# Sparse attention and FFN on one core: in units 14 to 23 the transfer engine turns the probabilities of all four head pairs

## The chip, the cores and the metric

One core of a Trainium2 chip. The metric is device time in microseconds, the median of three runs. The engines are TensorE (PE), VectorE (DVE), ScalarE (ACT), GpSimd (POOL) and SyncE (SP), which here only issues transfers; 16 DMA engines carry them.

## What is computed

```python
B, H, S, D = q.shape                  # 4, 8, 768, 64
scores = scale * np.matmul(q, k.transpose(0, 1, 3, 2))
mask = np.abs(blk_i - blk_j) <= window            # blocks of 32, window 1
mask = mask | (blk_i == 0) | (blk_j == 0) | (blk_i == n_blocks - 1) | (blk_j == n_blocks - 1)
...                                               # and 3 sampled blocks per block of queries
scores = np.where(mask, scores, -1000000000.0)
attn = softmax(scores)
x = (attn @ v) as [3072, 512]
h = x @ w_in                                      # 512 x 2048
g = np.where(h > 0.0, h, np.exp(np.minimum(h, 0.0)) - 1.0)
out = g @ w_out                                   # 2048 x 512
```

## The kernel before

The 3072 tokens are 24 **units** of 128 (`u` = 0 to 23), four blocks of 32 queries each. Units 8 and 20 hold the first and last blocks of a pair of batches, which attend to all keys; a head pair there has three tiles of keys, elsewhere one. Two units together make the tokens of one round of the FFN, **U** = 0 to 11 (U = 10 has units 20 and 21). Numbers are kept as two fp16 parts, a high and a low one.

`attention(u, t, via)` does this for a unit: Q is loaded and turned (qT, and qS with halves swapped), keys are gathered (kG, on POOL) and rows of V (VT, loads on SP and an indirect one on POOL). Then, for each of the four head pairs `hp` and each of its tiles: the scores on PE (line 788, into s), the row maximum on DVE (799), the exponential on ACT (817, into e), the cast to fp16 (p, high part), the subtraction that gives the low part (822, the second half of p), the **turn** of p into pT, and the product with V on PE (837, into w or av), 32 matmuls for a tile. Sums of those go to x; after the last pair the unit is normed, cast and subtracted (xn) and turned into xT, on which the FFN works. There are two e tiles, two p tiles and four pT tiles.

`turn16` makes a turn in one of two ways. By "PE" it is eight 128x128 transposes on TensorE (line 385) into a PSUM tile (the tag av, or s in units 8 and 20), which ACT or DVE then copies to pT (lines 297 and 299). By "DMA" it is one transpose by the transfer engine that SP issues (line 377), from p in SBUF to pT in SBUF. Which way a pair goes is the middle entry of `via`: pairs with `hp < via[1]` go by PE. Before, that is 4 for units 0 to 3 and `PP` = 2 for all others; their Q and xn go by DMA.

`ffn(U, t)` has eight steps `f2`: two groups of 12 matmuls for h (line 885, 256 columns each), three operations for the activation on ACT and DVE (895, 897, 893), cast and subtraction to g, and two groups of 6 matmuls into o (line 908, 512 columns). At the end of a U two tiles ro leave PSUM, and SP stores them (642); a U has two such stores, and there is one ro tile.

No engine chooses its work at run time. `Plan.add` notes every operation with the engines it may run on and a due time; `Plan.order` lets a model of the chip run, starts on each engine the earliest due operation that is ready in the model, with assumed durations, and writes the instructions in that order. Attention of a U has due times 130 (`LEAD`) ahead of its FFN, so the operations of later units lie between the FFN's matmuls of earlier tokens. On the chip each engine, and SP, then works strictly in the written order and waits where something is not there yet. A turn by DMA stands in the model as 1.3 on SP, 2.4 of transfer and 2.5 until it has landed:

```python
        if via == "DMA":
            plan.add({"SP": 1.3}, t, lambda e: nc.sync.dma_start_transpose(dst(), flat(src.ap)),
                     r=[src], new=new, w=w, dma=2.4, name=name)
            return
...
                turn16(t + PITCH * hp + TURN, p, lambda pT=pT: pT.ap, "PE" if hp < via[1] else "DMA", new=[pT], name=f"pt{u}.{hp}", bank=bank)
```

Of the kernel before, what the change touches and what calls it, by code (L numbers as in the profile page):

```python
# [225 lines left out]
def kernel(  # L226
# [44 lines left out]
    def buf(tag, shape, dtype, pool=None):  # L271
        def make():
            made[0] += 1
            return (pool or sb).tile(
                shape, dtype, tag=tag, bufs=rooms[tag], name=f"{tag}{made[0]}")
        return Buf(tag, make)
# [203 lines left out]
    def zero_rows(prio):  # L480
        z = buf("st4", [P, 2 * RW], F16)
        plan.add({"POOL": 0.6}, prio, lambda e: nc.gpsimd.memset(z.ap[0:BLK, :], 0.0), new=[z], name="zero")
        for g in range(NPAIR):
            for n in (0, NB - 1):
                for d, xs in vd[g]:
                    def put(e, d=d, xs=xs, n=n):
                        nc.sync.dma_start(d.ap[n * BLK : (n + 1) * BLK, :], z.ap[0:BLK, 0 : RW * len(xs)])
                    plan.add({"SP": 0.45}, prio, put, r=[z], new=[d] if n == 0 else [],
                             w=[d] if n else [], dma=0.3, name=f"z{g}")
# [26 lines left out]
    def spare(prio, n):  # L516

        got = []
        for _ in range((n + 1) // 2):
            vt = Buf("VT", lambda: None)  # L520

            def take(e, vt=vt):
                vt.slot = next_slot()
                in_room["v", vt.slot] = None
            plan.add({"SP": 0.01}, prio, take, new=[vt], name="spare")
            for half in range(2):
                got.append((Buf(None, lambda vt=vt, half=half: VT[
                    :, 2 * vt.slot + half].rearrange("p b (h x) -> p b h x", x=VW)), [vt]))
        return got
# [46 lines left out]
    def keys(g, x, c, prio, via="DMA"):  # L576
        s, n = buf("st2", [P, H, D], F32), buf("n2", [P, H, 2, D], F16)
        plan.add({"SP": 0.45}, prio, lambda e: nc.sync.dma_start(
            s.ap, k[2 * g + x][:, c * P : (c + 1) * P, :].rearrange("h p d -> p h d")),
            new=[s], dma=1.35, name=f"k{g}.{c}")  # L580
        split(prio, s, n, lambda: n.ap[:, :, 0, :], lambda: n.ap[:, :, 1, :], KS, True, f"k{g}.{c}")
        turn16(prio, n, lambda: kT[x][:, :, c * P : (c + 1) * P], via, w=[kT_buf[x][c]],
               name=f"kt{g}.{c}")

    def values(g, c, prio):
        n = buf("st4", [P, 2, H, VW], F16)
        ends(n, prio, f"v1{g}.{c}")
        for x in range(2):
            s = buf("st2", [P, H, D], F32)
            plan.add({"SP": 0.45}, prio, lambda e, s=s, x=x: nc.sync.dma_start(  # L590
                s.ap, v[2 * g + x][:, c * P : (c + 1) * P, :].rearrange("h p d -> p h d")),
                new=[s], dma=1.4, name=f"v{g}.{c}")
            split(prio, s, n, lambda x=x: n.ap[:, x, :, D + 1 : VW - 1], lambda x=x: n.ap[:, x, :, 0:D],
                  VS, False, f"v{g}.{c}")
        pieces = {0: [(0, BLK, NB * BLK), (BLK, P, BLK)],
                  NKC - 1: [(0, P - BLK, c * P), (P - BLK, P, (NB + 1) * BLK)]}.get(c, [(0, P, c * P)])
        for p0, p1, row in pieces:
            def put(e, p0=p0, p1=p1, row=row):
                nc.sync.dma_start(
                    vd[g][0][0].ap[row : row + p1 - p0, :], n.ap[p0:p1].rearrange("p b h x -> p (b h x)"))  # L600
            plan.add({"SP": 0.45}, prio, put, r=[n], w=[vd[g][0][0]], dma=1.55 * (p1 - p0) / P, name=f"vs{g}.{c}")
# [324 lines left out]
    TWO, AHEAD, T, F0, LEAD, NPE = 6, 16.0, 58.0, 60.0, 130.0, 4  # L926
    WI, WID, F2, LAG = -100.0, 3.0, 4.5, 14.0
    V1, K1 = 70.0, 16.0
    QP, PP, XP = 0, 2, 0
    zero_rows(-480)  # L930
    room = [None, None, *spare(-490, 4)]
    for x in range(2):
# [8 lines left out]
    for U in range(NU // 2):  # L941
        t = F0 + T * U
        for u in (2 * U, 2 * U + 1):
            at = t - LEAD + (T / 2 if U else NEXT) * (u % 2)
            if u == NUP:
                for c in range(NKC):
                    for x in range(2):
                        keys(1, x, c, at - K1 + c, "PE")
                for c in range(NKC):
                    values(1, c, at - V1 + 5 * c)  # L950
            attention(u, at, ("PE", 4, "PE") if u < NPE else (("DMA", "PE")[QP], PP, ("DMA", "PE")[XP]))
        ffn(U, t)
    warm_up()
    tables()
# [30 lines left out]
```

## Time and profile before

| | us |
|---|---|
| median of three runs | 823.76 |
| the runs | 824.18, 820.37, 823.76 |
| span of the profiled execution | 807.9 |
| median less span | 15.9 |
| PE busy in the span | 711.3 |
| DVE, ACT, POOL busy | 506.4, 428.9, 392.7 |

The profile is one execution, and its span is counted from the first to the last instruction; the profiled execution's own whole time is not given apart from the runs, so the median stands for it. Busy times of PE are unions of matmuls that overlap in the array. A wait is put down to what ended it. SP and the DMA engines have no busy share of their own in the head of the page; what they do is read from the issues and from who waits for them.

### The profile page before, as it was taken

Reading aid. Unit: us, or ns where it says so; the run is one execution under the profiler, and the core shown is the slowest. Engines: PE = TensorE matmul, PEld = TensorE weight load, DVE = VectorE, ACT = ScalarE, POOL = GpSimd, SP = SyncE. Lnnn points to the kernel's source line nnn. Section 1 sums busy time; section 2 is a strip of 40 time slices with the busy share of each in tenths; the row PEclk is TensorE's granted clock in tenths of the full one; section 3 lists DMA queues with packets and bytes.
Section 4 is the critical chain, followed back from the end, with each engine's and each line's share of the span. In section 5 each row is a group of like instructions: output and inputs, shape, how many; then the busy total and the mean of one; then the engine's idle time right before and its main releaser. Section 6 shows DMA issues by size and latency. Waiting matters only on the chain.

```text
span 807.9 us, 26664 instructions
## 1 busy us (share of the span) xinstructions
PE 711.3 (88%) x11256; PEld 488.3 (60%) x11256; DVE 506.4 (63%) x854; ACT 428.9 (53%) x747; POOL 392.7 (49%) x600
## 2 busy tenths in 40 slices
PE   6445665999998999899899998999999999999993
PEld 3333553767657657567567656656667576566761
DVE  7689788998876747666478766647555566522210
ACT  4598777888545636355466525445345346322220
POOL 2587657687534347543565535445324464422120
PEclk8555578999999999999999999999999999999997
DMA  8898999988787789999459987464761698210000
GB/s 231 248 281 277 264 263 212 217 204 163 134 179 223 169 148 209 172 170 200 94 106 182 162 176 93 110 131 42 172 114 15 94 208 146 41 40 1 28 1 26
DMA packets 191064, 120.07 MB, mean 149 GB/s; under 512 B 148000, under 2 KB 168608, under 8 KB 190944
## 3 DMA queue, kind: packets, MB, share of 16 engines
q1 hardware_dynamic: 185664, 100.79, 61.0%
q0 software_dynamic: 5280, 17.58, 8.5%
q8 instruction: 88, 1.44, 0.8%
q14 instruction: 32, 0.26, 0.1%
HBM read 82.05 MB, written 13.21 MB: 118 GB/s over the span
## 4 chain that ended last, share of the span: by engine, by line
PE 66%; DMA 14%; DVE 6%; issue 4%; ACT 3%; POOL 2%; SPq 2%; POOLq 1%; DVEq 0%; ACTq 0%
PE o L908 27%; PE h L885 25%; PE s L788 5%; DMA out_dram<-ro 5%; PE w L837 3%; DMA pT<-p 2%; PE av L837 2%; DMA wo<-in_moe_w_out_dram 2%; DMA st<-in_k_dram 2%; PE av L385 2%; DMA VT<-vd 1%; PE s L385 1%; DMA st<-in_v_dram 1%; ACT e L817 1%; DVE w L451 1%
## 5 line engine op out<-in xcount | busy, mean ns | idle before, releaser
L885 PE MATMUL h<-xT,wi 128*128 128x256 f16 x2304 | 280.4, 275 | 7.8 <-DVE fe L893 4.7
L908 PE MATMUL o<-wo,g 128*128 128x512 f16 x1152 | 274.6, 381 | 0.0
L885 PEld LDWEIGHTS <-wi 128*128 128x128 f16 x2304 | 220.2, 98 | 53.9 <-issue 9.0
L902 POOL TENSOR_TENSOR g<-fe,g 128x512 f16<-128x512 f32 x79 | 96.0, 1215 | 188.8 <-DVE g L299 167.8
L908 PEld LDWEIGHTS <-g 128*128 128x128 f16 x1152 | 107.5, 98 | 109.2 <-issue 1.6
L822 POOL TENSOR_TENSOR p<-e,p 128x512 f16<-128x512 f32 x86 | 102.3, 1193 | 88.6 <-DVE p L299 44.9
L895 ACT ACTIVATE fe<-h 128x512 f32<-128x512 f32 x96 | 57.3, 597 | 148.4 <-PE h L885 145.7
L893 DVE SCALAR_TENSOR_TENSOR fe<-h,fe 128x512 f32<-128x512 f32 x96 | 66.0, 688 | 107.8 <-ACT fe L897 100.1
L817 ACT ACTIVATE e<-s,m 128x256 f32<-128x256 f32 x208 | 86.1, 471 | 68.4 <-POOL p L822 25.4
L757 POOL COPY kG<-kT 128x128 int32 x264 | 76.3, 331 | 41.6 <-PE s L788 18.6
L799 DVE TENSOR_REDUCE m<-s 128x2 f32<-128x512 f32 x104 | 69.8, 685 | 36.0 <-PE s L788 35.7
L735 POOL DMA_INDIRECT VT<-vd,idx x66 | 65.5, 992 | 27.6 <-issue 9.1
L837 PEld LDWEIGHTS <-pT 128*32 128x32 f16 x3456 | 42.8, 97 | 47.3 <-issue 34.6
L897 ACT ACTIVATE fe<-fe,gs 128x512 f32<-128x512 f32 x96 | 69.3, 722 | 2.4
L788 PE MATMUL s<-kG,qT 128*32 128x160 f16 x704 | 44.5, 249 | 10.6 <-ACT e L817 6.3
L788 PEld LDWEIGHTS <-qT 128*32 128x32 f16 x1664 | 33.2, 101 | 28.9 <-issue 21.5
L846 DVE TENSOR_REDUCE x<-w 128x130 f32<-128x260 f32 x64 | 27.2, 425 | 33.6 <-PE w L837 33.2
L788 PE MATMUL s<-kT,qS 128*32 128x96 f16 (+1 forms) x832 | 48.2, 226 | 0.0
L788 PE MATMUL s<-kT,qT 128*32 128x96 f16 (+1 forms) x832 | 48.1, 227 | 0.0
L788 PE MATMUL s<-kG,qS 128*32 128x160 f16 x704 | 44.2, 248 | 4.0 <-DVE qS L299 2.7
L299 DVE CAST p<-e 128x512 f16<-128x512 f32 x54 | 32.4, 603 | 19.2 <-ACT e L817 6.3
L385 PEld LDWEIGHTS <-p 128*128 128x128 f16 x512 | 34.5, 105 | 15.9 <-POOL p L822 7.7
(134 smaller groups left out, 859.9 us busy)
## 6 DMA issues: line engine op xcount, KB each, us to landing
VT<-vd SPq DMA_DIRECT2D x44, 195.0 KB
VT<-vd SPq DMA_DIRECT2D x22, 390.0 KB
wo<-in_moe_w_out_dram SPq DMA_DIRECT2D x12, 512.0 KB
out_dram<-ro SPq DMA_DIRECT2D x21, 256.0 KB
st<-in_q_dram SPq DMA_DIRECT2D x40, 128.0 KB
wo<-in_moe_w_in_dram SPq DMA_DIRECT2D x9, 512.0 KB
st<-in_moe_w_in_dram SPq DMA_DIRECT2D x7, 512.0 KB
VT<-vd SPq DMA_DIRECT2D x12, 260.0 KB
```

Of the source, the lines that this page charges most:

```text
L735: nc.gpsimd.indirect_dma_start(VT[0:96, 2 * vt.slot, xs[0] : xs[-1] + 1].rearrange("p b x -> p (b x)"), None, d.ap, bass.IndirectOffsetOnA ...
L757: nc.gpsimd.tensor_copy(dst[:, :, r * 16 : (r + 1) * 16], src[:, :, bass.ds(at[r], 16)])
L788: nc.tensor.matmul(dst, lhsT=qq.ap[:, h, j * BLK : (j + 1) * BLK], rhs=mv, start=first, stop=(y == 1 and qq is qS and o0 + w == 256))
L799: nc.vector.tensor_reduce(m.ap[:, 2 * c : 2 * c + 2] if sp else m.ap[:, 6:8], ss[c].ap, axis=AX.X, op=ALU.max, negate=True)
L817: nc.scalar.activation(e32.ap[:, y, :], ss[c].ap[:, y, :], AF.Exp, bias=m.ap[:, 6 + y : 7 + y])
L822: plan.add(LO, t + PITCH * hp + 1, margin=MO, fn=lambda e, e32=e32, p=p: ENG[e].tensor_tensor(p.ap[:, 1, :], flat(e32.ap), p.ap[:, 0, :], ...
L837: nc.tensor.matmul(av.ap[j * BLK : (j + 1) * BLK, y, v0:], lhsT=pts[c].ap[:, pl * 4 + y * 2 + z, j * BLK : (j + 1) * BLK], rhs=VT[:, room, ...
L885: nc.tensor.matmul(h.ap[:, a, :], lhsT=w[:, wl, cs], rhs=x.ap[:, xl, cc, :], start=(n == 0), stop=(n == 3 * NCC - 1))
L893: nc.vector.scalar_tensor_tensor(e32.ap, h.ap, -IH * GS, e32.ap, op0=ALU.mult, op1=ALU.min)
L897: plan.add({"ACT": 0.68}, p0 + 2.6, lambda e, e32=e32: nc.scalar.activation(e32.ap, e32.ap, AF.Relu, bias=gs_col, scale=-GS), r=[e32], w=[ ...
L902: plan.add(LO, p0 + 2.6, margin=MO, fn=lambda e, e32=e32, g=g: ENG[e].tensor_tensor(g.ap[:, 1], e32.ap, g.ap[:, 0], op=ALU.subtract), r=[e ...
L908: nc.tensor.matmul(o.ap, lhsT=g.ap[:, gl, f % 2, m * P : (m + 1) * P], rhs=wo[f][:, wl, :], start=(f == 0 and n == 0), stop=(f == NFC - 1 ...
```

## The change

A constant says from which unit on no pair goes by PE. For units 14 to 23 `via[1]` becomes 0 in place of 2.

```diff
     QP, PP, XP = 0, 2, 0
+    TURNED = 14
...
-            attention(u, at, ("PE", 4, "PE") if u < NPE else (("DMA", "PE")[QP], PP, ("DMA", "PE")[XP]))
+            attention(u, at, ("PE", 4, "PE") if u < NPE else (("DMA", "PE")[QP], PP if u < TURNED else 0, ("DMA", "PE")[XP]))
```

Since the model sets the order, everything behind the first such turn is written anew, on every engine.

TensorE, at the first pair of unit 14, before: p810 is turned into the PSUM tile av814 (a pair of rows stands eight times) ahead of the product with pT799 of unit 13.

```order
L885 MATMUL h812_9903<-xT661_8039,wi_68 128x256
L385 LDWEIGHTS p810_9865
L385 MATMUL av814_9919<-ident16_76,p810_9865 128x128
...
L837 LDWEIGHTS pT799_9712
L837 MATMUL w816_9932<-VT_67,pT799_9712 32x130
```

The same place of TensorE in the change:

```order
L885 LDWEIGHTS wi_68
L885 MATMUL h812_9903<-xT661_8039,wi_68 128x256
...
L837 LDWEIGHTS pT799_9712
L837 MATMUL w818_9942<-VT_67,pT799_9712 32x130
```

The turn of p810 is gone from TensorE, and a further group of 12 matmuls for h stands ahead of the product. SP at that place before (xT, out and VT are the turn of xn, an output store and a load of V rows):

```order
L642 DMA st2808_9858<-in_q_dram 32x8x64 x4
L730 DMA VT_67<-vd17_191 96x2080 x2
L377 DMA_TRANSPOSE xT787_9566<-xn823_10037 128x8x128
L642 DMA out_0_dram<-ro818_9981 2x64x512
L377 DMA_TRANSPOSE pT839_10194<-p821_10025 128x8x128
L377 DMA_TRANSPOSE pT844_10255<-p828_10085 128x8x128
```

and in the change:

```order
L642 DMA st2808_9858<-in_q_dram 32x8x64 x4
L377 DMA_TRANSPOSE pT814_9919<-p810_9865 128x8x128
L642 DMA out_0_dram<-ro816_9938 2x64x512
L377 DMA_TRANSPOSE pT821_10013<-p813_9917 128x8x128
L730 DMA VT_67<-vd17_191 96x2080
L377 DMA_TRANSPOSE xT787_9566<-xn827_10066 128x8x128
L377 DMA_TRANSPOSE pT837_10162<-p833_10131 128x8x128
L377 DMA_TRANSPOSE pT844_10259<-p839_10177 128x8x128
```

p810 now goes through SP, ahead of the output store; the turn of the second pair stands behind that store, and the loads of V and the turn of xn (xT787) behind both. SP where units 21 to 23 run, before (pT1191 and pT1198 are unit 21's, pT1230 and pT1242 unit 22's, and xT1185 is for U = 10):

```order
L377 DMA_TRANSPOSE pT1191_14777<-p1181_14692 128x8x128
L377 DMA_TRANSPOSE pT1198_14836<-p1190_14775 128x8x128
...
L642 DMA out_0_dram<-ro1176_14643 2x64x512
L730 DMA VT_67<-vd17_191 96x2080 x2
L377 DMA_TRANSPOSE pT1230_15237<-p1219_15159 128x8x128
L377 DMA_TRANSPOSE xT1185_14713<-xn1225_15226 128x8x128
L642 DMA out_0_dram<-ro1226_15228 2x64x512
L377 DMA_TRANSPOSE pT1242_15417<-p1227_15230 128x8x128
```

and in the change (pT1188 and pT1199 are unit 21's, pT1205 to pT1233 unit 22's, pT1242 unit 23's, xT1178 is for U = 10):

```order
L377 DMA_TRANSPOSE pT1188_14784<-p1176_14661 128x8x128
...
L377 DMA_TRANSPOSE pT1199_14932<-p1194_14869 128x8x128
L377 DMA_TRANSPOSE pT1205_15050<-p1201_14936 128x8x128
L730 DMA VT_67<-vd17_191 96x2080 x2
L377 DMA_TRANSPOSE xT1178_14697<-xn1215_15179 128x8x128
L377 DMA_TRANSPOSE pT1223_15287<-p1209_15108 128x8x128
L377 DMA_TRANSPOSE pT1227_15334<-p1216_15181 128x8x128
L642 DMA out_0_dram<-ro1228_15360 2x64x512
L377 DMA_TRANSPOSE pT1233_15428<-p1230_15376 128x8x128
L642 DMA out_0_dram<-ro1238_15501 2x64x512
L377 DMA_TRANSPOSE pT1242_15524<-p1234_15430 128x8x128
```

Twice as many turns of p stand there in SP's row, and one output store stands before the last turn of unit 22, another before the first of unit 23. In TensorE's order the last product of unit 21 now stands nearer to the first h of U = 10; the matmuls between the two are counted in the prediction.

## Rows read from the trace of the kernel before

**Rows 1.** The page: span, and each engine's busy time in us.
```profile
span 807.9 us, 26664 instructions
PE 711.3 (88%) x11256; PEld 488.3 (60%) x11256; DVE 506.4 (63%) x854; ACT 428.9 (53%) x747; POOL 392.7 (49%) x600
```

**Rows 2.** Windows: stretch, length, busy us of PE, PEld, DVE, ACT, POOL, clock, DMA share, GB/s.
```profile
440.00:480.00 40.00, 40.00 (x666) 24.99 (x664) 28.04 (x50) 18.16 (x32) 20.62 (x27) 1.00 0.92 171
480.00:705.00 225.00, 216.46 (x3663) 147.85 (x3661) 130.79 (x229) 107.29 (x193) 103.33 (x138) 1.00 0.61 109
```

**Rows 3.** Waits of PE, 440 to 705 us: total us, times, longest.
```profile
PE h L885 <- DVE g L299: 3.0, 1, 3.0
PE w L837 <- DMA pT<-p: 2.5, 2, 1.4
...
PE av L837 <- DVE pT L299: 0.6, 1, 0.6
```

**Rows 4.** Tile pT, 440 to 705 us: durations in ns, least, median, most.
```profile
L377 SPq DMA_TRANSPOSE pT<-p x24: 1231/1281/5028, 446.3 to 694.4; - x24
L297 ACT ACTIVATE pT<-av x15: 1002/1023/1032, 442.3 to 691.6; 128x1024 f16<-128x1024 f16 x15
L299 DVE COPY pT<-av x3: 691/692/692, 439.4 to 670.7; 128x1024 f16<-128x1024 f16 x3
```

**Rows 5.** Chain of waits, 540 to 560 us: start, us, what.
```profile
535.89 8.00 DMA out_dram<-ro
...
545.36 9.02 DMA pT<-p
...
556.37 0.46 PE w L837 x32
...
559.54 0.45 PE av L385 x8
```

**Rows 6.** Windows of line 385 alone, then of line 788: PE, PEld.
```profile
480.00:705.00 225.00, 11.93 (x160) 10.03 (x160) 1.00 0.61 109
...
480.00:705.00 225.00, 22.54 (x1088) 17.28 (x1088) 1.00 0.61 109
```

**Rows 7.** Waits of SP's queue, 440 to 705 us: its longest in total.
```profile
SPq L377 <- POOL p L822: 61.9, 11, 22.1
```

**Rows 8.** Timeline: two issues with their product with V; a product that waited.
```profile
623.82 3.39 SPq L377 DMA_TRANSPOSE pT<-p  x2
...
630.16 0.53 PE L837 MATMUL av<-VT,pT 128*32 128x130 f16 x32
...
487.44 5.50 SPq L377 DMA_TRANSPOSE pT<-p  x2
...
499.05 0.53 PE L837 MATMUL w<-VT,pT 128*32 128x130 f16 x32
...
688.57 0.53 PE L837 MATMUL w<-VT,pT 128*32 128x130 f16 x32 [1.44 <-DMA pT<-p]
```

**Rows 9.** Chain of waits, 705 to 765 us: FFN alone.
```profile
710.30 7.87 PE h L885 x72
...
743.83 9.06 PE o L908 x42
```

**Rows 10.** Timeline: the last product with V, and the turns behind it.
```profile
703.19 0.54 PE L837 MATMUL w<-VT,pT 128*32 128x130 f16 x32
...
700.13 8.17 SPq L377 DMA_TRANSPOSE xT<-xn  x2
```

**Rows 11.** The page's groups: subtraction and cast of p; busy us, mean ns.
```profile
L822 POOL TENSOR_TENSOR p<-e,p 128x512 f16<-128x512 f32 x86 | 102.3, 1193 | 88.6 <-DVE p L299 44.9
...
L299 DVE CAST p<-e 128x512 f16<-128x512 f32 x54 | 32.4, 603 | 19.2 <-ACT e L817 6.3
```

## The prediction

> **What bounds the kernel now.** I read the page's head first: TensorE (PE) is busy for 711.3 of the 807.9 us span, more than any other engine [rows 1]. A mean hides stages, so I cut the stretch in which units 14 to 23 run. From 440 to 480 us PE is busy for 40.00 of 40 us at clock 1.00, from 480 to 705 us for 216.46 of 225 us; the 16 DMA engines are busy for 0.92 and 0.61 of the time, DVE and ACT for about half [rows 2]. So PE sets the end here, and work that leaves PE brings the end nearer unless a new wait takes its place. Then I asked what PE waits for between 440 and 705 us: 3.0 us once for a VectorE cast of the FFN, 2.5 us in two waits for turns by the transfer engine, 0.6 us once for the copy of a turn out of PSUM [rows 3]. All its idle time in 480 to 705 us is 225 − 216.46 = 8.5 us.
>
> **What the change removes.** Units 14 to 23 are nine ordinary units with two pairs each turned on PE, and unit 20, whose pairs have three tiles: 9 × 2 + 2 × 3 = 24 turns, as many as the 15 + 3 copies out of av plus six in unit 20 [rows 4]. Each is eight 128x128 matmuls. On the chain one costs 0.45 us until the next group takes over [rows 5]; the busy time of the line, which counts the last matmul's way through the array, is 11.93 us for 160, or 0.60 us a turn [rows 6]. The chain counts what PE is held for, so I take 0.45: **−10.8 us**, with 24 × 0.60 = 14.3 us as the far bound. The 24 copies (1.02 us on ACT, 0.69 on DVE [rows 4]) lie on engines that are half idle; I cost their removal at nothing, since PE hides them, apart from the one wait of 0.6 us that ends with them [rows 3]: **−0.6 us**.
>
> **What it adds.** 24 more transposes on SP's queue. SP is held for 1.28 us by one in the median [rows 4], 31 us in all over some 265 us. SP works in order, and a turn that waits there for its p holds back what stands behind it: loads of V, of Q, stores. SP already stood 61.9 us in 11 waits for the subtraction that completes p [rows 7], and PE had next to no wait for those loads, so I cost the holding back at nothing; its cover is that they are issued a unit ahead. If that cover goes, a V load that comes late stops the products with V of the next unit.
>
> The wait that counts is that of PE for a pT. In this stretch 24 turns go by DMA already. From issue on SP to the product with V on PE it took from 6.3 us (623.82 to 630.16) to 11.6 us (487.44 to 499.05) in all 24 [rows 8], and in only two of them did PE stand still: 2.5 us in all [rows 3], one of them for 1.44 us [rows 8]. The other is the turn of 545.36 us, issued just behind an output store; it took 9.02 us, and the store before it 8.00 us [rows 5]. That is 0.10 us a turn; at the same rate 24 more cost **+2.5 us**. The bounds: nothing, if the order's other PE work covers all; 24 × 1.25 = 30 us, if each waited as long as those two. I take the rate of the 24, the nearest row.
>
> DMA time: 480 to 705 us leaves 0.39 × 225 = 88 us free, which 20 of the turns fill only at 4.4 us each; two issues together took SP 3.39 us [rows 8]. From 440 to 480 us only 0.08 × 40 = 3.2 us is free, and units 14 and 15 bring four turns there, but PE has no idle time in it at all [rows 2], so PE runs on what was made ahead. I cost that at nothing.
>
> **What it moves.** The written order places attention later against the FFN. Between the last product with V of unit 21 and the first FFN matmul on its tokens (U = 10) stood 108 h and 90 o matmuls, and now stand 24 h, 48 o, one product and two score groups. At 7.87/72 = 0.109 us an h and 9.06/42 = 0.216 us an o [rows 9], 0.46 us a product [rows 5] and 22.54/34 = 0.66 us a score group [rows 6] that is 14.8 us of cover. What must fit beneath: the last product starts at 703.19 and the second xT is issued at 708.30 − 1.23 = 707.07 us [rows 4, 10], 3.9 us, and then 6.3 to 11.6 us until use [rows 8]: 10.2 to 15.5 us. So 0 to 0.7 us of new wait; I take **+0.4 us**. For U = 11 the cover is 48 h and 66 o, 19.5 us, and nothing is left over.
>
> The sum: −10.8 − 0.6 + 2.5 + 0.4 = −8.5 us. The profiled execution spans 807.9 us; the median of the runs, 823.76, stands 15.9 us above that, for what lies around the span, and the change leaves that alone. 823.8 − 8.5 = **815.3 us**.
>
> **The rivals.**
>
> *The waits eat the gain (same).* If eight of the 24 new turns wait as the two did (1.25 us each), that is 10 us instead of 2.5, and the time is 822.8 us. For: the 9.02 us came behind an output store, two of which come with every U, and a turn that lands late holds its p, so that casts on ACT and DVE stand in line with FFN work behind them. Against: the two waits in 24.
>
> *Attention falls behind (slower).* There are two p tiles. A tile turned on PE is free after 0.45 us; one turned by DMA only when the transfer has read it. In units 20 to 23 all 24 turns in a row now go that way, and the order gives them, from the first product to the last, 420 h, 210 o, 23 products and 15.5 score groups: 45.9 + 45.3 + 10.6 + 10.3 = 112 us, or 4.87 us a turn. A loop through one p is cast 0.60, subtraction 1.19 [rows 11] and the turn; two such loops run side by side. With the turn at 9.02 us [rows 5] that is 5.4 us, 0.5 us over, and 23 × 0.5 = 12 us: there the gain is gone, and that is the deciding point. At 10.3 us, midway to the slowest, it is 6.0 us a turn, 27 us of waiting, and 823.8 − 11.4 + 27 = 839 us. Against: 9 us are reached only behind a store; the use at 6.3 us after issue bounds the other turns from above and gives 4.1 us. The Trainium skill (VectorE: DVE Perf Modes, "The three transpose paths" and "Rules for kernel authors") speaks for this rival: it gives the crossbar 1309 ns for a 128x128 block, TensorE 390 ns, and says to use TensorE where PSUM will do as the destination. By an estimate from that page a turn of eight blocks is 10.5 us of transfer, one after another, and the change loses. The trace disagrees: 6.3 us from issue to use is less than 10.5, and two turns were issued within 3.39 us.
>
> *More than the sum (faster still).* At 0.60 us a turn and with no new waits: 823.8 − 14.3 − 0.6 = 808.9 us.
>
> *The change does nothing.* It is no rival: the order of the changed program holds 192 fewer transposes on PE and 24 more on SP.
>
> **How the numbers follow.** My forecast (809 to 819.6 us) 0.58, more than the sum 0.04, the eaten gain (819.7 to 827.9) 0.20, attention behind (above 827.9) 0.18. Half a percent, about what a measurement of this kernel can tell from no change, is 4.1 us. Faster 0.62, same 0.20, slower 0.18. The range begins at 809.5, just above the far bound of the gain, and reaches into the slower case to 830 us, so that about 0.15 of it is left out above and 0.05 below.
>
> **What the new profile would show.** If right: 576 in place of 768 transposes on line 385; 72 issues pT<-p; PE still over 95% busy from 440 us to the last product with V; waits for DMA pT<-p on PE of some 5 us in all; some 61 us of FFN alone behind the last product (240 h and 162 o in the order), against 90 now (384 and 222). Wrong in the first rival's way: four or more waits over 1 us, each behind a store. Wrong in the second's: PE idle between the products of units 20 to 23, with casts that wait for DMA pT<-p, and a gap before the first h of U = 10. The prediction falls if PE's idle time from 440 us on grows by more than 7 us.

## The result and the profile after

| kernel | median us | runs | ratio to before (95%) |
|---|---|---|---|
| before | 824.18 (819.25 to 827.85) | 15 | |
| changed | 816.94 | 15 | 0.9916 (0.9894 to 0.9939) |
| changed, beside the first experiments | 807.88 | 12 | 0.9953 (0.9927 to 0.998) |

The change gains 0.5 to 0.8%, and both intervals lie below 1; the kernel before took 812.86 us beside the second row. Ratios are of fast runs (of the 15 of the change, those of 825.72 and 1772.87 us are left out) and are not quite the quotients of the medians. The profiled execution of the change took 816.94 us with a span of 814.7, so 2.2 us lie around a span, not the 15.9 us that the prediction took: the execution whose rows stand above was a quick one beside the runs of its table, by some 14 us. Where it was quick is told by the timeline at the last product with V of unit 13, up to which both programs are almost the same; before, then after (start, us, what):

```profile
439.28 0.53 PE L837 MATMUL w<-VT,pT 128*32 128x130 f16 x32
```
```profile
449.71 0.53 PE L837 MATMUL w<-VT,pT 128*32 128x130 f16 x32
```

So spans must not be compared; the part from there to the last matmul may. The chains end with the last o group, before and after:

```profile
785.51 9.08 PE o L908 x42
```
```profile
792.25 9.08 PE o L908 x42
```

That part was 794.59 − 439.28 = 355.3 us and is now 801.33 − 449.71 = 351.6 us; in the second profile of the change (first experiment) 790.01 − 439.83 = 350.2 us. It gained 3.7 and 5.1 us, but not all by turns. The change does a group of 12 h matmuls (1.31 us on the chain) ahead of that product which the kernel before does behind it, and the first of the 24 turns stood ahead of it before. So 23 turns off PE gave 2.4 and 3.8 us here.

The windows after, against [rows 2], shifted by the 10 us (stretch, length, busy us of PE, PEld, DVE, ACT, POOL, clock, DMA share, GB/s):

```profile
450.00:480.00 30.00, 26.38 (x428) 17.44 (x413) 17.75 (x33) 11.94 (x24) 14.68 (x23) 1.00 1.02 147
480.00:740.00 260.00, 248.07 (x3927) 162.50 (x3926) 152.38 (x249) 100.74 (x193) 112.33 (x148) 0.99 0.80 129
```

The waits of PE from 450 us on, against [rows 3], and under them two of DVE's in the same stretch (total us, times, longest):

```profile
PE w L837 <- DMA pT<-p: 7.1, 5, 3.4
PE h L885 <- DVE fe L893: 3.9, 2, 3.2
PE av L837 <- DMA pT<-p: 2.8, 1, 2.8
PE h L885 <- issue: 1.5, 1, 1.5
...
DVE ro L301 <- DMA out_dram<-ro: 18.2, 3, 8.9
...
DVE p L299 <- DMA pT<-p: 11.8, 5, 3.4
```

Six waits for turns by DMA, 9.9 us, stand where there were two of 2.5; the DMA engines are at 0.80 to 1.02. The longest, on SP and then on PE (timeline):

```profile
448.76 0.60 SPq L642 DMA_DIRECT2D out_dram<-ro  x1
449.46 5.17 SPq L377 DMA_TRANSPOSE pT<-p  x1
...
463.22 0.53 PE L837 MATMUL w<-VT,pT 128*32 128x130 f16 x32 [3.38 <-DMA pT<-p]
```

The turn issued right behind an output store is used 13.8 us later. Three of the six waits, 6.6 of the 9.9 us, are for turns that stand right behind a store in SP's queue (issued at 449.46, 650.57 and 717.22 us). Of tile pT from 450 us on, against [rows 4]:

```profile
L377 SPq DMA_TRANSPOSE pT<-p x47: 1231/1780/6158, 449.5 to 731.2; - x47
```

No copy by ACT or DVE is left there, and SP is held for 1.78 us by a turn in the median, 1.28 before. The place where most is lost at once, on SP, DVE and PE (timeline):

```profile
707.52 0.56 SPq L642 DMA_DIRECT2D out_dram<-ro  x1
708.17 3.74 SPq L377 DMA_TRANSPOSE pT<-p  x1
...
715.87 0.69 DVE L301 TENSOR_SCALAR ro<-o 128x512 f32<-128x512 f32 x1 [5.13 <-DMA out_dram<-ro]
...
717.41 0.68 DVE L893 SCALAR_TENSOR_TENSOR fe<-h,fe 128x512 f32<-128x512 f32 x1
...
712.19 2.79 PE L885 MATMUL h<-xT,wi 128*128 128x256 f16 x24
718.15 4.28 PE L885 MATMUL h<-xT,wi 128*128 128x256 f16 x24 [3.17 <-DVE fe L893]
722.36 0.53 PE L837 MATMUL w<-VT,pT 128*32 128x130 f16 x32
```

An output store is issued at 707.52. The turn behind it is used at 722.36, 14.2 us after its own issue. DVE meanwhile stands 5.13 us for the one ro tile, which the store holds until it lands some 8 us after its issue, and the FFN operation in line behind that (893) makes PE wait 3.17 us. Directly after that wait the granted clock is 0.50, the lower of its two levels (1.2 GHz), from 717.9 to 721.1 us (window; the clock is the third figure from the end):

```profile
717.90:721.10 3.20, 2.95 (x14) 2.11 (x15) 3.10 (x5) 0.63 (x1) 2.40 (x2) 0.50 1.84 73
```

A row of 24 h matmuls took 2.79 us ahead of the wait and 4.28 us behind it, so the low clock cost 1.5 us.

### The profile page after: what moved, and what is told of

Its sections match the earlier page's. It is cut to its first block, busy times and chain, and to the rows that moved or that the text cites. A ratio compares the mean times of both kernels' runs of the same rounds, so it can differ in the third digit from the quotient of the medians.

```text
span 814.7 us, 26279 instructions
## 1 busy us (share of the span) xinstructions
PE 710.6 (87%) x11064; PEld 478.8 (59%) x11064; DVE 509.7 (63%) x851; ACT 407.6 (50%) x725; POOL 393.9 (48%) x601
## 4 chain that ended last, share of the span: by engine, by line
PE 58%; DMA 19%; DVE 7%; issue 6%; SPq 3%; ACT 3%; POOL 2%; POOLq 1%; another core or an unknown queue 1%; DVEq 0%; ACTq 0%
PE h L885 23%; PE o L908 23%; DMA pT<-p 10%; PE s L788 5%; PE w L837 3%; PE av L837 2%; DMA wo<-in_moe_w_out_dram 2%; DMA st<-in_k_dram 2%; PE av L385 1%; DMA out_dram<-ro 1%; DMA vd<-VT 1%; DMA st<-in_v_dram 1%; PE s L385 1%; SPq L377 1%; DMA VT<-vd 1%
## 5 line engine op out<-in xcount | busy, mean ns | idle before, releaser
L885 PE MATMUL h<-xT,wi 128*128 128x256 f16 x2304 | 285.0, 276 | 10.9 <-DVE fe L893 8.0
L885 PEld LDWEIGHTS <-wi 128*128 128x128 f16 x2304 | 220.7, 99 | 61.3 <-issue 10.3
L822 POOL TENSOR_TENSOR p<-e,p 128x512 f16<-128x512 f32 x94 | 112.1, 1195 | 115.3 <-DVE p L299 61.3
L902 POOL TENSOR_TENSOR g<-fe,g 128x512 f16<-128x512 f32 x69 | 83.2, 1206 | 140.2 <-DVE g L299 121.5
L757 POOL COPY kG<-kT 128x128 int32 x264 | 78.2, 339 | 52.1 <-PE s L788 29.8
L837 PE MATMUL w<-VT,pT 128*32 128x65 f16 (+1 forms) x2048 | 34.4, 208 | 7.4 <-DMA pT<-p 7.1
```

Source lines behind the costliest of these rows:

```text
L757: nc.gpsimd.tensor_copy(dst[:, :, r * 16 : (r + 1) * 16], src[:, :, bass.ds(at[r], 16)])
L822: plan.add(LO, t + PITCH * hp + 1, margin=MO, fn=lambda e, e32=e32, p=p: ENG[e].tensor_tensor(p.ap[:, 1, :], flat(e32.ap), p.ap[:, 0, :], ...
L837: nc.tensor.matmul(av.ap[j * BLK : (j + 1) * BLK, y, v0:], lhsT=pts[c].ap[:, pl * 4 + y * 2 + z, j * BLK : (j + 1) * BLK], rhs=VT[:, room, ...
L885: nc.tensor.matmul(h.ap[:, a, :], lhsT=w[:, wl, cs], rhs=x.ap[:, xl, cc, :], start=(n == 0), stop=(n == 3 * NCC - 1))
L902: plan.add(LO, p0 + 2.6, margin=MO, fn=lambda e, e32=e32, g=g: ENG[e].tensor_tensor(g.ap[:, 1], e32.ap, g.ap[:, 0], op=ALU.subtract), r=[e ...
```

## The experiments

"Before" is the kernel before, timed on the same chip. Waits are PE's from unit 14 on.

**1. The change once more.**

> The changed kernel once more, for a second profile beside its first. Its first profile has 9.9 us of PE idle time that ended with a turn by DMA behind unit 13, against 2.5 us before. The theory (24 turns of 0.45 us leave PE, new waits give some back): the ratio to before is 0.988 to 0.995 again, and the waits of PE for DMA pT<-p from unit 14 on are 5 to 12 us in total. A rival (the two profiles differ by chance in their first half, and the gain is an accident of that): the waits fall under 4 us or the ratio goes to 0.997 or more.

Ratio 0.9953 (0.9927 to 0.998). The waits:

```profile
PE w L837 <- DMA pT<-p: 5.5, 5, 2.5
PE h L885 <- DVE fe L893: 3.9, 2, 3.2
PE av L837 <- DMA pT<-p: 2.7, 1, 2.7
```

8.2 us for DMA, six waits again: they belong to the order, not to one execution. The ratio is a little above the expected range, and not at the rival's 0.997, though its interval reaches to 0.998.

**2. PE time put back.**

```diff
                 def times_v(e, c=c, hp=hp, av=av, pts=pts):
+                    if TURNED <= u and not sp and hp < 2:
+                        dead = ps.tile([P, 8, P], F16, tag="av", bufs=rooms["av"], name=f"dead{u}_{hp}")
+                        for i in range(8):
+                            nc.tensor.transpose(dead[:, i, :], ident16, ident16)
```

> The changed kernel, with eight transposes of the identity on PE, into a PSUM tile that nobody reads, ahead of the product with V of the first two pairs of the nine ordinary units from 14 on: 18 turns' worth of PE time put back, with nothing else in the order moved and no copy out of PSUM. The theory, by which PE time sets the end: 18 x 0.45 = 8.1 us more than the changed kernel, less the part that falls into waits for pT (up to 3 us): 5 to 8 us, ratio to before 0.997 to 1.002. The rival, that the pace of the turns by DMA sets the end and PE waits anyway: under 2 us more, ratio 0.991 to 0.994.

811.92 us, ratio 0.9996 (0.9965 to 1.0027): within the ratio of the theory, though only 4.0 us over the change beside it (807.88) instead of 5 to 8. The waits say where most of the rest of 8.1 us went (line numbers are shifted by the edit):

```profile
PE av L841 <- DMA pT<-p: 3.8, 2, 2.8
PE h L889 <- DVE fe L897: 3.4, 2, 2.7
PE w L841 <- DMA pT<-p: 1.7, 1, 1.7
```

PE waits 5.5 us for turns instead of 8.2, and all its waits together are 9.1 us instead of 12.7: 3.6 us of the dead work run where PE stood. PE time does set the end, except in those waits.

**3 and 6. The transfers alone, with and without p.** In the kernel before, SP issues a transpose beside each of the 24 turns on PE; in 6 it reads weights in place of p (`flat(wi[0])` for `f`).

```diff
         def go(e):
             f = flat(src.ap)
+            if name[:2] == "pt" and int(name[2:].split(".")[0]) >= 14:
+                dead = sb.tile([P, 8, P], F16, tag="st4", bufs=rooms["st4"], name=f"dead{name}")
+                nc.sync.dma_start_transpose(dead, f)
```

> The kernel before, in which the 24 turns of units 14 to 23 stay on PE, and SP issues a transpose by DMA of the same p beside each, into a tile that nobody reads. PE waits for none of them, but they hold p until it is read, fill SP's queue and the DMA engines as the change does. The theory (the transfers themselves cost little, the waits of PE for pT are what is given back): 0 to 3 us more than before, ratio 1.000 to 1.004. The rival, by which the load on the queue and the held p tiles are the cost: 5 us or more, ratio 1.006 or more.

860.28 us, ratio 1.0586 (1.054 to 1.0632): a clear miss of the theory, 47 us over before.

> The kernel before with 24 transposes by DMA beside the turns on PE, as in the third experiment, at the same places of SP's queue and of the same size, but reading a tile of weights that nobody writes, in place of p. The third cost 48 us, and its profile shows casts that wait up to 12.5 us for a p which such a transpose still reads. If the held p was the cost: under 10 us more than before, ratio 1.000 to 1.012. If the load on SP's queue and the DMA engines was: 30 us or more, ratio over 1.035.

831.82 us, ratio 1.025 (1.0202 to 1.0297): between the two expectations. Windows of 3, then of 6:

```profile
480.00:705.00 225.00, 198.75 (x3166) 132.76 (x3169) 112.88 (x201) 89.96 (x163) 87.32 (x121) 0.93 0.70 118
```
```profile
480.00:705.00 225.00, 207.80 (x3495) 140.64 (x3494) 123.55 (x218) 98.60 (x180) 98.95 (x135) 0.97 0.84 133
```

Casts that wait in 3 (two of many such rows), then in 6:

```profile
DVE p L299 <- DMA deadpt14.1_10031<-p: 12.5, 1, 12.5
ACT p L297 <- DMA deadpt15.1_10537<-p: 7.7, 1, 7.7
```
```profile
DVE p L299 <- DMA pT<-p: 11.6, 3, 7.1
ACT p L297 <- DMA pT<-p: 11.0, 3, 4.5
```

So 24 more transposes that nobody waits for cost 2.5%, about 20 us, when they read weights, and 3.4%, about 27 us, more when they read p. In 3 they then hold one of two p tiles and also wait on SP until p is complete, with the queue behind them; no run parts these two. Both orders had been made as if p were free after a turn on PE. The clock falls too, and is part of both costs: 0.93 and 0.97 where the kernel before had 1.00 [rows 2]. The change issues as many transfers and is faster than before; what differs is that its order was made with them in the plan, and that PE, ACT and DVE have less to do. No run shows how much is due to which.

**4 and 11. Output stores in two halves.**

```diff
-            parts = [(far[b : b + 2, i * BLK : (i + 2) * BLK], tile_)]
+            parts = [(far[b + x, i * BLK : (i + 2) * BLK], tile_[64 * x : 64 * x + 64]) for x in range(2)]
```

> The changed kernel with each output store of an ordinary unit issued as two transfers of 64 rows x 2 KB, in place of one of 2 x 64 rows. In the first profile an output store takes 8 to 11 us from issue to landing, and turns behind it 9 us and more. If the stores hold the turns back: a store lands in under 5 us, the waits of PE for DMA pT<-p fall from 9.9 us to under 5, and the ratio to before to 0.980 to 0.987. If something else makes the turns late (the load of the DMA engines, or when p is ready): the waits stay at 7 us or more and the ratio at 0.988 to 0.995.

768.2 us, ratio 0.9451 (0.942 to 0.9482): 45 us under before (812.86), where the change beside it gained 5. The written order is that of the change.

> The kernel of the fourth experiment once more (changed, split stores), now on the same chip as the next one. Ratio to before 0.942 to 0.950, with no idle time of PE of over 2 us behind unit 13, if that result was not one of its chip.

768.67 us, ratio 0.9457 (0.941 to 0.9503), again without a wait of PE behind unit 13: it repeats. The windows behind unit 13 (fourth experiment):

```profile
430.00:480.00 50.00, 50.00 (x766) 32.73 (x764) 34.12 (x58) 20.53 (x40) 24.51 (x40) 1.00 0.93 167
480.00:700.00 220.00, 220.00 (x3497) 145.03 (x3496) 133.63 (x223) 89.73 (x173) 101.88 (x129) 1.00 0.70 134
```

PE has not one wait left, with as many turns by DMA as in the change. Read from the semaphores in the traces, a store from 445 to 720 us landed 7.8 to 10.3 us after its issue in the change, a half store from 428 to 680 us 2.2 to 5.7 us here. Against the second profile of the change, the part behind unit 13 is 16.6 us shorter. Most of the gain beyond the expectation lies where the change does nothing: the part up to unit 13 is 11.5 us shorter (its last product starts at 428.33, not 439.83), and behind the last matmul the last store lands sooner. The end of the fourth's chain:

```profile
752.84 9.08 PE o L908 x42
```

Its span is 766.9 us, so 5.0 us follow the last matmul; before and in the second profile of the change, 13.3 us did (794.59 in a span of 807.9, 790.01 in 803.3). The Trainium skill (DMA: Bandwidth & Descriptors, "Why a DMA increments its semaphore by 16 and not by 1") says that a transfer takes as many engines, up to 16, as divide the outermost size of both its sides. For a store of 2 x 64 rows that is 2 engines by the rule, for one of 64 rows 16. The landing times above agree, and a whole store raises its semaphore in 3 steps, a half in 16; which engines carried it no view here shows.

**5. The kernel before with split stores.**

> The kernel before, with the output stores issued as two transfers of 64 rows each, as in the fourth experiment. There the same edit took 0.945 of the time and no idle time of PE was left behind unit 13. If PE time is what the change saves and the stores were what gave it back: the split before has no waits either but 24 turns more on PE, 24 x 0.47 = 11 us more than the split change: ratio to before 0.956 to 0.962, and the change is then worth 1.2 to 1.6%. If the turns by DMA are cheap only because the order was planned anew, or PE has other slack: a difference of under 6 us between the two, ratio under 0.953.

781.93 us, ratio 0.9609 (0.9578 to 0.964).

```profile
430.00:480.00 50.00, 49.76 (x866) 33.28 (x864) 33.78 (x59) 25.43 (x47) 25.96 (x42) 1.00 0.82 163
480.00:700.00 220.00, 218.82 (x3497) 148.30 (x3495) 126.31 (x222) 101.80 (x181) 97.20 (x126) 1.00 0.51 105
```

The change is worth 781.93 − 768.2 = 13.7 us, or 1.6 points of the ratio, once stores are short: the upper end of what was expected. From the last product of unit 13 to the last matmul the two take 772.51 − 425.75 = 346.8 and 761.92 − 428.33 = 333.6 us. Of these 13.2 us, 1.4 are waits of the kernel without the change, 1.3 the group of 12 h that the change does ahead of that product (1260 and 1249 matmuls of line 885 in the part), and 10.5 are the 23 turns behind it: 0.46 us each.

**7. Stores from ScalarE's queue.** `nc.scalar.dma_start` for `nc.sync.dma_start` where `move` stores.

> The changed kernel with its output stores unsplit but issued from ScalarE's queue, so that no turn stands behind a store in SP's queue; the one ro tile is held by the store as before. If the queue is what makes a store delay the turns: the waits of PE for DMA pT<-p fall from 8 to 10 us to under 3, those of DVE for DMA out_dram<-ro stay at 15 us or more, and the ratio goes to 0.955 to 0.985. If it is the transfer itself (two DMA engines that the store holds, which each transpose needs too): the waits of PE stay at 6 us or more and the ratio at 0.985 or more.

812.83 us, ratio 0.999 (0.9967 to 1.0014).

```profile
PE h L885 <- DVE fe L893: 6.8, 3, 3.6
PE o L908 <- ACT ro L297: 4.5, 1, 4.5
...
PE w L837 <- DMA pT<-p: 0.7, 1, 0.7
...
DVE ro L301 <- DMA out_dram<-ro: 18.7, 3, 8.9
ACT ro L297 <- DMA out_dram<-ro: 10.2, 2, 8.4
```

Of the waits for turns, 0.7 us are left: it is the place behind a store in SP's queue that made those turns late. The time is no better, a miss of that expectation's ratio. The store still holds ro, DVE and ACT stand for it, and PE waits for them instead. A long store reaches PE by two ways, and closing one is not enough; experiment 4 closes both.

**8, 10 and 12. Turns by DMA from an earlier unit, with split stores.** `TURNED = 4`, and twice `TURNED = 12`.

> The changed kernel with split stores and with the turns by DMA from unit 4 on in place of unit 14: 24 more turns off PE (units 4 to 7 and 9 to 13 two each, unit 8 six). The split change keeps PE busy all of the time behind unit 13. If PE time sets the end in units 4 to 13 too: 24 x 0.47 = 11 us less, 757 us, ratio to before 0.930 to 0.934. If the DMA engines are the bound there (0.95 busy from 300 to 400 us): no gain or a loss, ratio 0.945 or more, with idle time of PE between 200 and 430 us.

802.76 us, ratio 0.988 (0.9843 to 0.9917): slower than with unit 14, as in the second case. From 300 us on the split change had 128.91 of 130 us, this one (second row) loses 11 us of 140:

```profile
300.00:430.00 130.00, 128.91 (x2223) 91.30 (x2223) 91.65 (x155) 75.87 (x132) 77.11 (x122) 1.00 0.92 170
```
```profile
300.00:440.00 140.00, 129.06 (x2049) 87.86 (x2047) 87.97 (x145) 68.03 (x123) 74.61 (x120) 0.95 0.90 179
```

But the DMA engines are no busier in it (0.90 against 0.92), and PE's longest wait there in total is for exponentials, not for turns (waits, 200 to 440 us):

```profile
PE s L788 <- ACT e L817: 8.8, 4, 3.2
```

That the DMA engines are the bound in these units is not shown; the cause of the loss stays open.

> The changed kernel with split stores and the turns by DMA from unit 12 on. From unit 4 on it was 4.3 points slower than from 14 on. If units 12 and 13, the first of the second pair of batches, still have room on the DMA engines: four turns fewer on PE, 1.9 us less, ratio to before 0.941 to 0.945. If they have none (0.92 busy from 300 to 430 us): ratio 0.947 or more, with idle time of PE between 380 and 440 us.

787.67 us, ratio 0.9561 (0.9515 to 0.9607), but with before at 826.01 us; so it was run again beside the other:

> The kernel of the tenth experiment (turns by DMA from unit 12 on, split stores) once more, beside the one from unit 14 on. It had 0.956 against 0.945, but in another call, in which the kernel before took 826 us instead of 813. If units 12 and 13 cost time: 0.5 to 1.2 points above the run beside it. If the difference was that of the two calls: within 0.4 points of it, or below it by the 1.9 us of four turns.

773.69 us, ratio 0.9515 (0.9471 to 0.9559), 5.0 us over experiment 11 on the same chip, and the runs of the two do not overlap (772.96 to 775.19 against 767.1 to 769.76). Four turns more by DMA cost more than they save. Its PE waits are one of 2.3 us between 380 and 460 us, for which the profile shows no releaser, and one of 2.9 us for an xT behind; from 300 to 430 us the DMA engines are as busy as in experiment 11 (0.91 and 0.90). So it is not shown that units 12 and 13 lack room on them.

**9. Four p tiles.**

```diff
-buf("p", [P, 2, 512], F16)
+buf("st4" if u >= TURNED and c_all(u, hp, c) % 2 else "p", [P, 2, 512], F16)
```

`c_all` numbers a unit's tiles. The order is planned anew with them, so it is not quite that of the change.

> The changed kernel with four p tiles in place of two for units 14 to 23: every second tile of a unit takes the place of a staging tile that is idle by then. The stores stay unsplit. If it is the stores that give the gain back: the waits of PE for DMA pT<-p stay at 6 us or more, and the ratio to before at 0.988 to 0.998. If a p held by its transfer is what makes attention late in the change (the slower rival of the prediction, in part): the waits fall under 3 us and the ratio to 0.985 or less.

819.88 us beside 826.01, ratio 0.9927 (0.9898 to 0.9956).

```profile
PE s L791 <- issue: 6.1, 3, 3.3
PE w L840 <- DMA pT<-p: 4.0, 1, 4.0
PE w L840 <- issue: 3.7, 1, 3.7
PE h L888 <- issue: 1.6, 2, 0.8
```

The time is that of the change, as the stores' theory has it; the waits for turns fell to one of 4.0 us, between the two expectations, and others, for which the profile shows no releaser, took their place. This run alone does not show that held p tiles are not the limit of the change; in experiment 4 two p tiles are enough for PE to wait for nothing once stores are short.

## Why the prediction was right

Forecast 815.3 us in 809.5 to 830 and faster; measured 816.94, ratio 0.9916. The sign and the mechanism held: PE time that leaves PE shortens the kernel, and new waits give part of it back. The term of the waits was too small. That the time came within 1.7 us is in part luck: the forecast's ratio, 815.3 / 823.8 = 0.990, lies in the first interval but below the second (0.9927 to 0.998), and the part that the change touches gained only 2.4 and 3.8 us by its 23 turns.

- **The turns (−10.8 us).** Right: 0.46 us a turn where nothing else interferes (4 against 5), 10.9 us for 24. The 0.45 of the chain was the right price, the busy time of 0.60 too high.
- **The waits of PE for pT (+2.5 us).** Undersized: all waits for turns went from 2.5 to 9.9 and 8.2 us, so 24 more turns cost 5.7 to 7.4 us. The failing step is "at the same rate": a rate per turn from a queue in which two of four went by DMA does not hold when all four do. From unit 14 to the last product, six of eleven stores now have a turn as the next entry in SP's queue, four of nine did before, and one such pair was in the order shown ahead of the prediction (pT821, behind the store at unit 14): that is the longest wait. This is the rival in which waits eat the gain, and it took more than half of it. (The 8.00 us of [rows 5] are those of the store issued at 535.89; the turn of 545.36 stands behind another, issued at 544.71. That changes no term.)
- **DMA time in 440 to 480 us, "at nothing".** PE stood for 30 − 26.38 = 3.6 us from 450 to 480, at a DMA share of 1.02. But 3.4 of them are the wait behind the store shown above, already counted in the 9.9. With split stores the same turns left PE no wait there (50.00 of 50 us, at 0.93): it was the store and not DMA time as a whole. Idle-free PE before was no proof of cover.
- **xT of unit 21 (+0.4 us).** No wait for it appears. At U = 10 PE waited instead for DVE, behind the ro tile (3.17 us): a cause that the prediction did not name, although the chain already held an 8.00 us store [rows 5].
- **The base.** 15.9 us around the span was wrong (2.2). It did no harm, since the sum is a difference added to the median.
- **Attention behind (the slower rival)** did not happen: the pace of the turns never held PE once stores were short. Where the order does not plan for them, transfers that read p cost 47 us in experiment 3, some 27 of them because they read p. By the estimate from the Trainium skill (VectorE: DVE Perf Modes, "The three transpose paths"), 10.5 us of transfer a turn and one after another, 48 turns would take 504 us. The trace disagrees: with split stores the part with the 48 products took 333.6 us, and PE waited for none.
- **The signs.** The 72 issues and the FFN alone behind the last product (61.4 us) came as forecast. PE was busy for 94.6% from 450 to 740 us, not over 95%, and the waits for turns were 9.9 us, not 5. Four of them were over 1 us, the number of the first rival, two of these right behind a store. PE's idle time grew by 6.3 us, just under the 7 at which the prediction was to fall.

Of the 10.5 us of 23 turns, 2.4 and 3.8 stayed in the two profiles. More idle time of PE accounts for 6.3 us in the first (15.5 after, 9.2 before, all waits of PE added) and 3.5 in the second (12.7). The rest, 1.8 and 3.2 us, is nearly all the lower clock behind long waits. The first profile has one stretch of it, the 1.5 us shown above. The second has two: behind a wait of 3.18 us the 24 h took 4.46 us, and behind one of 2.73 us a product took 0.93 in place of 0.53 and the 24 h behind it 3.73 us, against 2.79 at the higher level: 3.0 us together.

The fastest kernel here is the changed one with split stores: 768 us, 5.5% under before.

## What to carry to other kernels

When work moves from the engine that bounds to a queue, do not price the new waits at the rate of the old ones; look at what each new entry stands behind in that queue. A stall that shows up as "DMA a <- b" may belong to the transfer ahead of it: here a store whose outermost size was 2 held a queue, a tile and, through them, three engines. And as many transfers cost 47 us in an order made without them, beside the turns that stayed on PE, and paid off in one made with them and without those turns. So an added transfer is better tried with the schedule made anew, though no run here parts the two.

## What the runs showed that was not expected

- Cutting each output store from one transfer of 2 x 64 rows into two of 64 rows took 3.9% off the kernel before (781.93 us), whose PE seemed 96% busy in the part looked at, and 4.9% off the change (807.88 to 768.2 us): in its spans 11.5 us up to unit 13, 16.6 behind it and 8.3 at the end.
- Behind a wait of 3.17 us the granted clock fell to 0.50 from 717.9 to 721.1 us in the change, where PE had been at 1.00 for over 300 us. It did not behind another of 3.38 us, at 460 us.
- The same kernel before had medians of 812 to 826 us in different sittings, a spread twice the change's gain; only ratios beside it on one chip could tell the change.
